# Batch 0's q and k turned by products, batch 1 scored unpaired, and the list in a new order

## The chip, the cores and the metric

The kernel runs on 1 core of one Trainium2 chip. The metric is the device time of one execution in microseconds; the runs shown are compared by their median.

## The reference

```python
def _attn_ref(q, k, v):                 # 8 batches, 8 heads, 576 tokens, 64 dims
    scores = scale * np.matmul(q, k.transpose(0, 1, 3, 2))
    mask = np.abs(pos[:, None] - pos[None, :]) <= 32
    scores = np.where(mask, scores, -1000000000.0)
...                                     # softmax over keys, times v
def _moe_ref(x, w_gate, wq, wk, wv, wo):   # x: 8 x 576 x 512, the heads side by side
    logits = x @ w_gate                    # 4 experts, the best 2 per token, softmax of these
    for e in range(4):
        q = x @ wq[e]; k = x @ wk[e]; v = x @ wv[e]     # 64 wide
        ...                                # causal attention
        ye = a @ v @ wo[e]
        ...                                # added where e is chosen, times its weight
```

So each batch has a sliding window attention of 8 heads and then a mixture of four causal attentions of one head each.

## The kernel before

The kernel is a list of some thousand steps (`ORDER`), written out by hand or by a planner, and each step is a small function that issues a few instructions. The order of the list is the order in which each engine gets its instructions; what overlaps across engines is decided by semaphores alone. A step's name holds the operation, then batch, and then what it needs: `sc210@24` is operation sc of batch 2, head group 1, half 0, with PSUM banks from 2 and from 4; a letter behind a colon names the engine of a copy (v VectorE, a ScalarE, g GpSimd) or, for products, whether the rows are split (q) or not.

The steps that matter here, for a batch b and a group g of four heads:

- `lq`, `lk`, `lv` load q, k and v. Loads go to the SP queue (f: ScalarE's queue), and `load` makes each wait for the last product ahead of it in the list. For batch 0, q and k come in two parts of 8 and 10 of the 18 tokens of a partition.
- `tq`, `tk` turn q and k with VectorE's stream transpose (line 317), in blocks of 32. Each head then has its 64 dims as two blocks of 32 rows. `mv` moves such blocks within SBUF by four DMAs (line 366), and `qc`, `kc` copy one block by an engine, so that a product can take 64 rows at once. `PAIRED` says whether that was done: a paired score block has 20 products of 64 rows, an unpaired one 40 of 32 rows.
- `hq`, `hk` turn batch 0's q and k on TensorE instead (line 193), two tokens at a time, and `iq`, `ik` copy the result from PSUM (lines 182 and 184), by 64 partitions.
- `sc` makes the scores of one half of the queries for four heads. For batches in `NBS` it adds the mask beforehand, by 8 products with the unit matrix. `ex` is the exponential (line 418). For other batches `mk` multiplies by the mask afterwards (line 422).
- `vc` copies v rows to the other 64 partitions' layout; `av` multiplies with v; `un` normalises on VectorE (lines 450 to 457); `xt` turns the result (line 193), `xf` and `xb` copy and cast it.
- `ga` to `gu` are the gate. `pp`, `pe`, `pv`, `ve` make the experts' q, k and v; `ps`, `xe`, `se` their scores, exponential and causal mask (lines 618 to 623); `po`, `oe`, `pt`, `ot` their products with v; `py`, `ye`, `st` the output.
- `wm` are dummy products, four to a step, that fill the time before data arrives (line 237).

Scores of batch b + 1 or b + 2 are interleaved by the list with the experts' work of batch b.

Of the kernel before, what the change touches and what calls it, by code (L numbers as in the profile page):

```python
# [25 lines left out]
NBS = (0, 1)  # L26
OCUT = 8

ORDER = """
    lq002:e s_mask s_ones s_fill s_ident s_warm s_pads lq001:e lk001:f lq012:e wm2@0 lk002:f lk012:f wm0@0 lq011:e  # L30
    lv02 lk011:f hq001@0 lv00 wm3@2 lv03 iq0013:v@0 lk100:e iq0012:a@0 iq0010:v@0 hq000@2 iq0003:v@2 iq0000:a@2
    iq0001:a@2 hk000@3 ik0003:a@3 iq0011:a@0 ik0002:a@3 s_nb hq011@4 iq0113:v@4 iq0110:v@4 iq0112:v@4 iq0002:v@2
    ik0001:a@3 hk001@6 wm1@0 ik0010:a@6 ik0000:v@3 hk011@0 iq0111:v@4 hq010@2 iq0100:v@2 iq0101:v@2 lv01 vc01:g
    ik0111:v@0 lq100:e ik0110:v@0 lv04 lk110:e ik0012:a@6 ik0113:v@0 lq110:e lw1 ik0013:a@6 iq0102:v@2 ik0011:a@6
    sc001@35 ex0010@3 hk010@7 ik0100:a@7 iq0103:a@2 ik0101:a@7 ik0112:v@0 ex0011@5 sc000@02 ik0103:v@7 ex0001@2
    ik0102:v@7 sc011@46 ex0110@4 sc010@24 ex0111@6 ex0101@4 lw0 av03@4 tk100:e kc10:v ex0100@2 ex0000@0 av04@0
    tq100:e un03@4 qc10:a mv10 vc00:g un04@0 lk200:e av02@2 lq200:e un02@2 lv13 xt02@4 xf02:a@4 xt01@2 av00@0
    xf01:a@2 tq110:e xb01:g xb02:g un00@0 av01@4 un01@4 xt00@4 xf00:a@4 lv10 cw0:g tk110:e sc101@02 qc11:a kc11:v
    sc100@46 mv11 tk200:e ex1010@0 ex1000@4 ex1001@6 lv11 ex1011@2 xb00:g lv12 ga0@0 gt0 gm0 ge0 cw1:g gu0@0
    pp011@4 pe011:a@4 pp010@2 lk210:e pe010:a@2 tq200:e pp000@6 ps011@2 pe000:a@6 qc20:v ps013@4 xe011@2 se011  # L40
    vc11:v pp001@0 pe001:a@0 xe013@4 kc20:g lq210:e ps010:q@6 se013 mv20 lv14 sc111@02 lq300:e xe010@6 sc110@46
    ex1111@2 tk210:e ex1110@0 ex1101@6 ps002:q@2 ps003:q@0 xe003@0 se010 ps001:q@6 ex1100@4 lw2 xe001@6 ps000:q@0
    xe000@0 vc10:g av11@4 un11@4 xe002@2 av10@6 un10@6 ps012:q@0 xe012@0 lv22 kc21:a sc201@24 se012 lk300:e
    ex2010@2 mk2010:g tq210:e cw2:g ex2011@4 qc21:a mv21 sc200@06 xt10@2 ex2001@6 xf10:a@2 tq300:e qc30:a av12@4
    av13@6 pv01@2 lv23 av14@3 xb10:g ve01:a@2 se003 ex2000@0 lq310:e un12@4 un13@6 xt11@6 xf11:a@6 xb11:a mk2011:g
    un14@3 lk310:e tk300:e kc30:g pv00@0 ve00:a@0 xt12@6 xf12:v@6 xb12:g se001 mk2001:v sc210@24 mv30 ex2100@2
    mk2000:v lv21 sc211@06 ex2111@6 lw3 lq400:e ex2110@0 mk2110:g ga1@3 ex2101@4 gt1 ge1 pv10@6 ve10:a@6 mk2101:g
    se002 gm1 gu1@3 pp100@4 tk310:e lv24 mk2111:g pe100:a@4 lv20 pp110@2 pe110:a@2 sc300@04 ex3001@4 ex3000@0 lv31
    sc301@26 tq310:e lk400:e pp101@4 ex3010@2 pe101:v@4 ex3011@6 cw3:a se000 po00@0 oe00@0 ps100@4 xe100@4 ps101@6
    xe101@6 po01@2 pt00@0 oe01@2 ot00:a@0 vc20:g qc31:g pp111@4 kc31:g mv31 pe111:a@4 lv32 lv33 ps102@6 mk2100:g  # L50
    vc21:g pt01@0 se100 ps103@1 xe103@1 xe102@6 se102 tq400:e qc40:g ps110@4 xe110@4 se110 pv11@3 ve11:a@3 av23@1
    av20@6 ot01:v@0 un23@1 mk3011:g py02@5 ye02:a@5 av24@0 lq410:e ps113@1 xe113@1 lk410:e un20@6 tk400:e ps112@4
    xe112@4 un24@0 ps111@6 xe111@6 py01:q@2 av21@4 un21@4 av22@6 un22@6 ye01:a@2 se113 sc311@02 ex3111@2 sc310@46
    tq410:e ex3110@0 kc40:g mv40 st02 mk3001:g ex3101@6 se112 ex3100@4 lk500:e mk3010:g xt20@2 xf20:a@2 xt21@0
    xf21:a@0 xt22@6 lv30 xf22:v@6 se101 se103 po10@4 oe10@4 py00@2 ye00:a@2 sc400@06 ex4000@0 st01 ex4001@6
    lq500:e mk3101:g lv42 sc401@24 xb20:g ex4011@4 se111 po11@0 lv34 lk510:e qc41:g ex4010@2 pt10@7 xb22:v xb21:g
    tk410:e pp201@5 pe201:a@5 pp200@2 kc41:a lv41 ga2@6 pe200:a@2 ps200@2 tk500:e ps203@4 st00 xe203@4 mv41 oe11@0
    ps202@0 xe202@0 xe200@2 ot10:v@7 pt11@7 ot11:a@7 gt2 pp210@4 mk3100:v mk3000:g vc31:g pe210:v@4 tq500:e
    pp211@0 mk3110:g mk3111:g av33@2 pv21@7 un33@2 vc30:g av31@4 un31@4 lq510:e mk4010:g qc50:g ve21:a@7 pe211:a@0
    ge2 lv43 av34@7 un34@7 py11:q@0 ye11:a@0 mk4001:g py10:q@2 ye10:a@2 py12@7 ye12:a@7 av30@4 gm2 gu2@6 av32@0  # L60
    xt32@6 un30@4 xf32:a@6 sc410@24 un32@0 kc50:g mv50 xb32:g lv52 mk4011:v ex4101@4 mk4101:g ex4100@2 mk4100:g
    sc411@06 ex4110@0 tq510:e qc51:g mk4110:g lk600:e lv40 xt31@4 xf31:a@4 lq600:e se200 xb31:v xt30@2 xf30:a@2
    pv20@0 ve20:v@0 ps213:q@2 ex4111@6 mk4111:g lv44 vc41:g xe213@2 se213 xb30:v tk510:e vc40:g ps212:q@4 xe212@4
    mk4000:g sc501@26 ex5010@2 ex5011@6 sc500@04 ex5000@0 lv53 mk5000:g tk600:e ex5001@4 pp300@2 pp301@0 pe300:a@2
    kc51:a se203 ps201@4 xe201@4 tq600:e pe301:a@0 ps211@2 ga3@7 xe211@2 gt3 kc60:g mv51 gm3 pp311@5 pe311:a@5
    ps210@0 xe210@0 se210 lv51 ps302@2 xe302@2 se211 pv31@4 av42@5 un42@5 ge3 ve31:a@4 vc50:g av43@0 un43@0 av40@2
    un40@2 ps301@5 xe301@5 lk610:e se301 av44@4 un44@4 qc60:a pp310@0 pe310:a@0 gu3@7 xt41@4 xf41:v@4 mk5010:g
    ps300@2 xe300@2 se202 av41@6 un41@6 ps303:q@0 sc511@24 xe303@0 mv60 se212 mk5001:v ex5110@2 ex5111@4 lq610:e
    sc510@06 lv54 lv50 mk5110:g tk610:e kc61:v lq700:e ex5101@6 ex5100@0 xt40@2 xf40:a@2 xb41:g xb40:g pv30@4
    ve30:a@4 xt42@0 xf42:v@0 sc600@26 ex6001@6 xb42:g ex6000@2 lk710:e mk5101:v sc601@04 ex6011@4 ex6010@0 lk700:e  # L70
    pp400@6 se201 po20@2 mk5011:g pe400:a@6 tq610:e qc61:g ps313@0 xe313@0 ps312@4 oe20@2 tq700:e ps311@6 xe311@6
    pp411@0 pt20@2 lq710:e xe312@4 ot20:a@2 pe411:a@0 mk5100:g po21@6 oe21@6 pp401@4 vc51:g ga4@3 mk5111:g
    pe401:a@4 ps403@6 xe403@6 ps401@4 xe401@4 ps310@0 xe310@0 tk700:e kc70:g mk6001:g pv41@2 ve41:a@2 av51@6
    un51@6 qc70:g gt4 ge4 av52@4 un52@4 av50@0 se310 pt21@2 ot21:a@2 se302 st11 un50@0 mv61 pv40@6 mv70 gm4
    ve40:a@6 xt50@4 gu4@3 mk6011:g ps402@0 av54@2 un54@2 lv60 xf50:a@4 xb50:g lv64 se401 av53@6 lv70 un53@6
    xe402@0 sc610@24 ex6100@2 lv62 ex6101@4 lv63 sc611@06 ps400:q@2 ex6111@6 xe400@2 tq710:e mk6101:g py21@4
    pp410@6 pe410:v@6 ex6110@0 ye21:a@4 lv61 st10 lv71 se402 xt51@2 xt52@0 xf52:v@0 xf51:a@2 se312 xb52:a mk6100:g
    sc701@46 ex7010@4 sc700@02 ex7001@2 xb51:v pp500@4 ex7000@0 mk6000:g tk710:e lv73 pp501@2 st12 ex7011@6 se303
    se313 se311 po31@6 oe31@6 lv72 pe501:a@2 pp511@2 pe511:v@2 st21 mk6111:g se300 po30@0 oe30@0 pe500:a@4 qc71:a
    ps503@6 ps502@4 xe503@6 mk6010:v xe502@4 ps411@2 xe411@2 vc60:g ga5@7 gt5 ps410@0 xe410@0 ps501@5 ge5 pt31@4  # L80
    ot31:v@4 pp510@2 pt30@4 pe510:v@2 mk6110:g kc71:g vc61:g py20@0 xe501@5 gm5 av61@2 av60@5 ot30:a@4 un61@2
    ye20:a@0 gu5@7 un60@5 av63@0 un63@0 av62@2 un62@2 py22@7 ye22:v@7 ps413@4 xe413@4 av64@6 mv71 sc711@04 un64@6
    ex7110@0 xt60@2 ex7111@4 se502 xt62@6 st22 lv74 xf62:v@6 xf60:a@2 xb60:v py31@0 mk7011:g sc710@46 ye31:a@0
    st31 ex7101@6 se413 mk7110:g ex7100@4 mk7100:v xt61@2 xf61:a@2 ps412@0 xe412@0 mk7111:g pv50@6 se501 st20
    se403 se400 po40@2 oe40@2 ga6@0 ve50:a@6 gt6 ps513@6 xe513@6 mk7001:g ps500@4 xb62:g ps510@2 xe500@4 pt40@1
    xb61:g xe510@2 vc71:v pp601@6 pe601:a@6 mk7000:g pp600@4 pe600:a@4 ge6 se410 ot40:v@1 se411 se412 po41@2
    pp611@4 pe611:a@4 py30@6 mk7010:g se500 ye30:a@6 pv61@1 py32@4 ye32:a@4 ve61:a@1 oe41@2 gm6 gu6@0 vc70:g
    av72@2 un72@2 ps602@6 xe602@6 ps600@4 av73@0 mk7101:g un73@0 av70@2 un70@2 xe600@4 ps603@6 ps601@4 xe603@6
    pt41@0 ot41:v@0 xe601@4 pp610@6 pe610:a@6 ps511@4 ps512@2 xe512@2 se601 se512 xe511@4 se510 st30 se503 av74@0
# [695 lines left out]
```

## Time and profile before

| | |
|---|---|
| median of 3 runs | 241.84 us (241.49 to 243.21) |
| the profiled execution: time, span | 240.19 us, 238.5 us |
| PE busy, instructions | 213.3 us (89%), 4579 |
| DVE busy | 188.1 us (79%) |
| ACT busy | 164.3 us (69%) |
| POOL busy | 144.7 us (61%) |
| DMA | 48.80 MB, mean 205 GB/s |

PE is TensorE's products, PEld its loads of weights, DVE VectorE, ACT ScalarE, POOL GpSimd. The span runs from the first to the last instruction of the profiled execution; its time has some 1.7 us more around it. The shares are means over a run whose stages differ, so a table by stretches of time says more than they do. Products are pipelined and their ends are modelled, so that a busy PE may still be issuing slowly: the count of instructions in a stretch is to be read beside the busy time.

### The profile page before, as it was taken

To read this page: it belongs to the slowest core of one execution; us is meant where nothing else is said; L and a number is where in the kernel's file an instruction comes from. 1 tells how busy PE (TensorE), PEld (TensorE's weight loads), DVE (VectorE), ACT (ScalarE), POOL (GpSimd) and SP (SyncE) were. 2 spreads that over 40 slices of the span, in tenths; PEclk is the share of its full clock that TensorE was granted. 3 is DMA by queue.
4 is the path that set the end of the run, shared out by engine and by line. 5 is a ranking of instruction groups with operands and counts; after the bars stand their busy time and mean duration, and the time that the engine had idled before them with its cause. 6 is when DMAs were issued, how large, how long until landed. Compare 5 with 4: busy or idle time off the path is not lost.

```text
span 238.5 us, 10662 instructions
## 1 busy us (share of the span) xinstructions
PE 213.3 (89%) x4579; PEld 166.9 (70%) x4588; DVE 188.1 (79%) x350; ACT 164.3 (69%) x260; POOL 144.7 (61%) x189
## 2 busy tenths in 40 slices
...
GB/s 208 289 286 304 222 279 205 280 276 252 270 240 258 236 210 324 275 233 201 287 160 185 176 322 278 166 214 197 205 16 160 55 108 4 73 133 0 201 200 198
DMA packets 57487, 48.80 MB, mean 205 GB/s; under 512 B 40544, under 2 KB 43104, under 8 KB 57440
## 3 DMA queue, kind: packets, MB, share of 16 engines
...
q10 hardware_dynamic: 576, 1.18, 1.5%
...
## 4 chain that ended last, share of the span: by engine, by line
PE 53%; DVE 14%; POOL 9%; DMA 8%; ACT 6%; issue 6%; SPq 1%; ACTq 0%; DVEq 0%; POOLq 0%
PE PS L190 49%; DMA T<-T 5%; DVE T L317 5%; PE PS L193 4%; POOL A L422 4%; DVE T L184 3%; DMA V<-in_v_dram 3%; ACT A L418 2%; ACT XTF L182 2%; POOL V L184 1%; POOL ATE L623 1%; DVE XN L451 1%; DVE OE L659 1%; SPq L196 1%; POOL XTB L184 1%
## 5 line engine op out<-in xcount | busy, mean ns | idle before, releaser
L422 POOL TENSOR_TENSOR A<-A,MASKP 128x576 f32<-128x576 f32 x40 | 57.6, 1448 | 7.7 <-ACT A L418 7.4
L623 POOL TENSOR_SCALAR_AFFINE_SELECT ATE<-ATE 128x256 bf16<-128x256 bf16 (+1 forms) x80 | 31.1, 407 | 37.2 <-ACT ATE L618 30.8
L618 ACT ACTIVATE ATE<-PS 128x1024 bf16<-128x1024 f32 x48 | 47.5, 1030 | 6.0 <-PE PS L190 6.0
L418 ACT ACTIVATE A<-PS 128x576 f32<-128x576 f32 x64 | 38.3, 653 | 16.7 <-PE PS L190 16.1
L190 PE MATMUL PS<-T 64*64 64x128 f32 (+3 forms) x1280 | 40.6, 263 | 2.7 <-DMA T<-T 1.3
L190 PE MATMUL PS<-V,A 128*64 128x65 f32 (+1 forms) x1280 | 39.5, 223 | 3.2 <-POOL V L184 1.7
L190 PEld LDWEIGHTS PS<-V,A 128*64 128x64 f32 (+1 forms) x1280 | 36.0, 132 | 7.5 <-POOL V L184 2.0
L190 PEld LDWEIGHTS PS<-T 64*64 64x64 f32 x1280 | 34.2, 133 | 6.2 <-DMA T<-T 1.4
L184 POOL COPY V<-V 64x1536 f32<-64x1536 f32 (+1 forms) x14 | 24.8, 1772 | 18.8 <-DMA kn<-in_k_dram 14.1
L317 DVE STREAM_TRANSPOSE T<-qn 128x1152 f32<-128x1152 f32 x14 | 32.6, 2329 | 4.5 <-DMA kn<-in_k_dram 1.9
L317 DVE STREAM_TRANSPOSE T<-kn 128x1152 f32<-128x1152 f32 x14 | 32.3, 2330 | 1.3 <-DMA T<-T 0.8
L451 DVE TENSOR_TENSOR XN<-PS,RC 128x512 f32<-128x512 f32 x32 | 22.1, 691 | 1.3 <-DVE RC L450 0.2
L182 ACT COPY Y<-PS 128x1024 f32<-128x1024 f32 (+1 forms) x20 | 16.7, 859 | 8.8 <-PE PS L190 5.7
L182 ACT COPY XTF<-PS 128x1024 f32<-128x1024 f32 (+1 forms) x21 | 17.2, 834 | 7.9 <-PE PS L193 6.3
L184 POOL CAST XTB<-XTF 128x128 bf16<-128x128 f32 (+1 forms) x21 | 15.5, 758 | 11.7 <-ACT XTF L182 11.3
L190 PE MATMUL PS<-WV,XTB 128*128 128x256 bf16 (+1 forms) x192 | 18.6, 256 | 2.0 <-DVE OTT L184 1.8
L190 PE MATMUL PS<-WO,OTT 128*128 128x512 bf16 (+2 forms) x99 | 18.4, 347 | 1.7 <-ACT OTT L182 1.1
L182 ACT CAST QKE<-PS 128x576 bf16<-128x576 f32 x25 | 15.9, 644 | 5.4 <-PE PS L190 5.2
L190 PE MATMUL PS<-QKE 64*128 64x64 bf16 (+9 forms) x220 | 17.9, 279 | 1.6 <-DVE OE L659 1.0
L190 PE MATMUL PS<-XTB,WK 128*128 128x288 bf16 x128 | 18.3, 286 | 0.1
L190 PE MATMUL PS<-XTB,WQ 128*128 128x288 bf16 x128 | 18.0, 286 | 0.0
L190 PEld LDWEIGHTS <-XTB 128*128 128x128 bf16 (+1 forms) x192 | 14.4, 102 | 5.1 <-issue 3.4
...
## 6 DMA issues: line engine op xcount, KB each, us to landing
...
kn<-in_k_dram SPq DMA_DIRECT2D x28, 288.0 KB, 5.4
qn<-in_q_dram SPq DMA_DIRECT2D x28, 288.0 KB, 5.1
T<-T SPq DMA_DIRECT2D x56, 144.0 KB, 4.2
...
```

Source lines behind the costliest of these rows:

```text
L182: nc.scalar.copy(o, i)
L184: eng(c).tensor_copy(o, i)
L190: last_pe[0] = nc.tensor.matmul(*a, **kw)
L193: last_pe[0] = nc.tensor.transpose(*a)
L196: r = q_.dma_start(o, i)
L317: nc.vector.transpose(T.rearrange("q h (p o) -> q h o p", o=18)[:, :, o0:o1, :], x[:, :, o0:o1, :])
L418: nc.scalar.activation(AT[(2 * b + g) % NAT_][half][p], two(b0)[:, :, 0:HS], EXP, scale=scale_att)
L422: eng(c).tensor_tensor(out=ap, in0=ap, in1=MASK[:, None, HS * half:HS * half + HS].to_broadcast([128, 2, HS]), op=MULT)
L451: nc.vector.tensor_tensor(out=XN[T // 2][:, T % 2, :].rearrange("p (t h d) -> p h t d", t=4, h=8), in0=u[:, :, 0:64].rearrange("p h (d t) ...
L618: nc.scalar.activation(chunk(A, ch), two(b0), EXP, scale=scale_moe)
L623: nc.gpsimd.affine_select(ap, ap, pattern=[[0, n], [1, w]], compare_op=IS_GE, fill=0.0, base=0, channel_multiplier=-1)
L659: nc.vector.tensor_tensor(out=O[:, :, :, :].rearrange("p t e d -> p e t d"), in0=p_[:, :, :, 0:64], in1=rg[:, :, :, None].to_broadcast([12 ...
```

## The change

The batch 0 turns become products with the unit matrix: for each token two products, of 64 columns each, put two heads into the lower and two into the upper 64 partitions of PSUM. Eight copies of 128 partitions take the place of 32 copies of 64. Batch 1 leaves `NBS`, so that its mask is applied by eight `mk` steps, and its `mv`, `qc` and `kc` steps are gone from the list, so that its scores are unpaired. The list is in another order throughout, with other engines for some copies; products without the split now carry the letter p.

```diff
-NBS = (0, 1)
+NBS = (0,)
...
     def hx(nm, b, g, ch, b0):
...
-        for n, oo in enumerate(range(4 * ch, 4 + 5 * ch)):
-            turn_pe(o[:, 128 * n:128 * n + 128], x[:, 2 * oo:2 * oo + 2, :].rearrange("p o d -> p (o d)"), ident)
+        for n, tok in enumerate(range(OCUT * ch, (OCUT, 18)[ch])):
+            for e in range(2):
+                mm(o[64 * e:64 * e + 64, 64 * n:64 * n + 64], x[:, tok, :], ident[:, 64 * e:64 * e + 64], start=True, stop=True,
+                   skip_group_check=True)
...
-    def ix(c, n, b, g, ch, k, b0):
-        e, p = k // 2, k % 2
-        m = 4 + ch
-        o = PS[64 * e:64 * e + 64, b0:b0 + 1 + ch, :].rearrange("p a x -> p (a x)")[:, 0:128 * m]
-        T = QKT[g][64 * p:64 * p + 64, 0:3:2, n, :].rearrange("q a (p oo e) -> q a p oo e", oo=9, e=2)
-        copy(c, T[:, :, :, 4 * ch:4 * ch + m, e],
-             o.rearrange("d (oo h p) -> d h p oo", oo=m, h=4)[:, 2 * p:2 * p + 2])
+    def ix(c, n, b, g, ch, b0):
+        lo, hi = ((0, OCUT), (OCUT, 18))[ch]
+        o = PS[:, b0:b0 + 1 + ch, :].rearrange("p a x -> p (a x)")[:, 0:64 * (hi - lo)]
+        T = QKT[g][:, 0:3:2, n, :].rearrange("q a (p o) -> q a p o", o=18)
+        copy(c, T[:, :, :, lo:hi], o.rearrange("d (o a p) -> d a p o", a=2, p=32))
```

The list's beginning, before and after, up to batch 0's last turn (`xt00`) and the first scores of batch 1:

```
before:
lq002:e s_mask s_ones s_fill s_ident s_warm s_pads lq001:e lk001:f lq012:e wm2@0 lk002:f lk012:f wm0@0 lq011:e
lv02 lk011:f hq001@0 lv00 wm3@2 lv03 iq0013:v@0 lk100:e iq0012:a@0 iq0010:v@0 hq000@2 iq0003:v@2 iq0000:a@2
...
sc001@35 ex0010@3 hk010@7 ik0100:a@7 iq0103:a@2 ik0101:a@7 ik0112:v@0 ex0011@5 sc000@02 ik0103:v@7 ex0001@2
ik0102:v@7 sc011@46 ex0110@4 sc010@24 ex0111@6 ex0101@4 lw0 av03@4 tk100:e kc10:v ex0100@2 ex0000@0 av04@0
tq100:e un03@4 qc10:a mv10 vc00:g un04@0 lk200:e av02@2 lq200:e un02@2 lv13 xt02@4 xf02:a@4 xt01@2 av00@0
xf01:a@2 tq110:e xb01:g xb02:g un00@0 av01@4 un01@4 xt00@4 xf00:a@4 lv10 cw0:g tk110:e sc101@02 qc11:a kc11:v
sc100@46 mv11 tk200:e ...

after:
lq001:e s_fill wm3@0 wm2@0 lq002:e s_warm s_ident lk001:f lq012:e lk002:f lk012:f lk011:f s_ones lv00 hq000@0
iq000:a@0 hq001@2 s_mask lv04 lq011:e s_nb iq001:a@2 hk000@0 ik000:a@0 lq100:e hq011@4 iq011:a@4 lv02 hk001@2
ik001:a@2 s_pads hk011@4 lv01 sc001@02 ex0010@0 ik011:v@4 lv03 ex0011@2 vc01:g sc000@46 ex0000@4 ex0001@6
tq100:e lw1 hq010@0 iq010:a@0 lk100:e tk100:e lw0 hk010@4 cw0:g ik010:a@4 sc011@02 ex0110@0 sc010@46 lk110:e
lq110:e ex0111@2 av03@2 un03@2 vc00:a av02@0 ex0100@4 un02@0 ex0101@6 av01@6 lv14 lv13 av04@5 un04@5 lq200:e
av00@2 xt02@0 xf02:a@0 un01@6 lk200:e xt01@4 xf01:a@4 xb01:g un00@2 xt00@2 xf00:a@2 xb00:g sc100@06 ex1001@6
ex1000@0 wm0@4 lv11 lv10 sc101@24 ex1011@4 ex1010@2 tk110:e lv12 xb02:g cw1:g pp010:p@0 pe010:a@0 tq110:e
...
ga0@7 mk1011:v ps013:p@0 ps010:p@5 xe013@0 mk1100:g ps011:p@3 xe011@3 wm1@2 xe010@5 pp000:p@0 mv20 pe000:a@0
...
```

More of the change, by code (lines that the diff above doesn't have):

```diff
@@ L25 @@
 NOE = 2
-NBS = (0, 1)
+NBS = (0,)
 OCUT = 8
 ORDER = """
[L30 to L89, printed above, removed]
-    un74@0 av71@6 pv51@0 un71@6 py42@1 ve51:a@0 st32 ye42:v@1 st42 xt72@2 xf72:a@2 xt71@4 xf71:a@4 xb72:g xt70@6
-    xf70:a@6 xb70:v xb71:v ps611@0 py41@2 py40@4 ye41:a@2 ye40:a@4 po50@6 xe611@0 pv60@2 ve60:a@2 pp700@0 se600
-    st41 oe50@6 ps610@6 xe610@6 pe700:v@0 se602 ps612@2 xe612@2 se513 st40 se511 po51@4 pp710@0 oe51@4 pt50@2
-    pp711@6 se611 se612 ot50:v@2 pe711:a@6 pt51@2 pe710:v@0 ot51:a@2 se603 po60@4 ps613@6 se610 xe613@6 se613
-    ps711@0 ps710@2 xe710@2 se710 xe711@0 pp701@6 pe701:a@6 oe60@4 pt60@4 po61@2 oe61@2 py50@0 ye50:a@0 st50
-    ot60:a@4 py51@6 ye51:v@6 ps702@2 py52@5 ye52:a@5 st51 pv71@0 ga7@1 ve71:v@0 gt7 xe702@2 se702 st52 ps701@6
-    ps703@2 xe703@2 ps700@4 se703 xe701@6 se701 xe700@4 pt61@0 ot61:v@0 pv70@2 gm7 py60@6 ge7 ye60:a@6 ve70:v@2
-    py61@4 st60 ye61:a@4 ps712@2 st61 xe712@2 se711 gu7@1 pw710@0 ow710@0 se700 po70@6 oe70@6 py62@4 ye62:a@4 st62
-    ps713@0 tw710@5 se712 pt70@6 ot70:v@6 pw711@7 ow711@7 uw710:a@5 py70@4 tw711@7 uw711:v@7 xe713@0 se713 pw712@6
-    ye70:a@4 st70 py71@0 ye71:a@0 st71 ow712@6 tw712@7 uw712:a@7 py72@7 ye72:v@7 st72
@@ new lines @@
+    av00@2 xt02@0 xf02:a@0 un01@6 lk200:e xt01@4 xf01:a@4 xb01:g un00@2 xt00@2 xf00:a@2 xb00:g sc100@06 ex1001@6
+    ex1000@0 wm0@4 lv11 lv10 sc101@24 ex1011@4 ex1010@2 tk110:e lv12 xb02:g cw1:g pp010:p@0 pe010:a@0 tq110:e
+    pp011:p@4 pe011:a@4 lq210:e lw2 mk1000:g tq200:e qc20:g sc110@02 ex1100@0 ex1101@2 tk200:e kc20:a mk1010:g
+    ga0@7 mk1011:v ps013:p@0 ps010:p@5 xe013@0 mk1100:g ps011:p@3 xe011@3 wm1@2 xe010@5 pp000:p@0 mv20 pe000:a@0
+    pp001:p@3 pe001:a@3 gt0 lk210:e lv24 ge0 sc111@05 ex1110@0 vc10:g vc11:g mk1001:v mk1101:v av11@3 gm0 gu0@7
@@ new lines @@
+    lv23 un11@3 lq300:e av10@0 un10@0 cw2:a ex1111@5 mk1111:g pv01@7 lk300:e ve01:a@7 sc200@24 ex2001@4 ex2000@2
+    sc201@06 ex2011@6 ex2010@0 tq210:e ps001:p@4 tk210:e xe001@4 xt10@2 lk310:e se013 mk1110:g xf10:a@2 ps000:p@6
+    xe000@6 kc21:g lv20 av12@0 un12@0 av13@4 ps012:p@2 xe012@2 se001 un13@4 av14@0 un14@0 tq300:e qc21:g mv21
+    ps002:p@6 lw3 xt11@4 xe002@6 se002 lv22 xf11:a@4 xt12@2 xf12:a@2 xb10:g xb12:g xb11:a pv00:p@0 ps003:q@4 ga1@2
+    mk2010:g tk300:e ve00:a@0 xe003@4 lv21 se003 gt1 ge1 pp100:p@6 gm1 mk2001:g pe100:a@6 gu1@2 pp101:p@4
@@ new lines @@
+    pe101:a@4 lq310:e sc210@06 sc211@24 ex2101@6 kc30:g qc30:v mv30 ex2100@0 ex2110@2 se000 se011 pp110:q@6 se010
+    ex2111@4 lq400:e tk310:e se012 po01@2 oe01@2 pe110:a@6 ps103:p@4 cw3:a xe103@4 ps102:p@6 xe102@6 lk400:e
+    po00@0 pp111:p@4 oe00@0 mk2000:g lk410:e pe111:a@4 pt01@7 mk2111:g ps101:q@2 ps100:q@0 xe101@2 tq310:e
+    ot01:v@7 pt00@6 xe100@0 pv10:p@4 ve10:v@4 ot00:a@6 lv31 mk2100:g ps113:p@0 ps110:p@2 xe113@0 mk2101:g xe110@2
+    sc300@06 ex3000@0 sc301@24 ex3001@6 ex3010@2 pv11@0 py02@1 se101 ve11:a@0 ex3011@4 lq410:e vc21:g qc31:g
@@ new lines @@
+    ps112:p@6 mk2011:v xe112@6 mk2110:g vc20:g lv33 se103 av23@2 tq400:e un23@2 py01:q@4 se102 kc31:a mv31
+    ps111:q@6 xe111@6 ye01:a@4 ye02:a@1 st02 tk400:e kc40:a se113 av24@0 se100 po10@2 oe10@2 mk3001:g av22@6 se110
+    py00:q@4 pt10@3 qc40:a un24@0 st01 un22@6 ot10:v@3 se112 se111 po11@0 oe11@0 av20@6 ye00:a@4 st00 mk3010:g
+    av21@4 un20@6 pt11@0 ot11:a@0 un21@4 mv40 sc310@26 ex3100@2 mk3011:g mk3000:v mk3100:g lk500:e sc311@04
+    tq410:e ex3101@6 ex3110@0 ex3111@4 py11:q@2 lq500:e lv30 py12@7 ye12:a@7 xt20@0 ye11:a@2 xt21@4 lv32 xf21:a@4
@@ new lines @@
+    mk3111:g qc41:g py10:q@6 xf20:v@0 xb20:g xb21:g xt22@2 xf22:v@2 lv34 ye10:a@6 lv41 xb22:a sc401@04 ex4010@0
+    mk4010:g tk410:e lv44 lk510:e sc400@26 ex4011@4 ex4000@2 pp200:q@0 pp201:q@2 ex4001@6 pp210:q@6 tk500:e
+    pe200:a@0 pp211:q@0 pe201:a@2 kc41:a pe210:a@6 ga2@2 vc31:a mk3110:g ps202:p@6 tq500:e gt2 gm2 ps200:p@3
+    pe211:a@0 mk3101:g av34@5 vc30:g av32@0 un34@5 ge2 gu2@2 un32@0 mk4011:g xe202@6 se202 mv41 xe200@3 qc50:a
+    lq510:e av31@6 av30@2 pv21@0 un31@6 kc50:g mv50 mk4001:g ve21:a@0 av33@4 xt32@6 xf32:a@6 un30@2 mk4000:g lv43
```

48 lines of the change are left out of this document (44 added, 4 removed).

## The prediction

> **What bounds the kernel now.** I read the table by stages first. Its columns are stretch and length in us, then busy us and instruction count of PE, PEld, DVE, ACT and POOL, the granted clock, the DMA share and GB/s.
>
> ```profile
> 12.00:30.00 18.00, 13.26 (x384) 11.28 (x384) 16.81 (x26) 9.57 (x18) 4.75 (x5) 1.00 0.95 272
> 30.00:60.00 30.00, 25.53 (x622) 20.94 (x622) 25.34 (x34) 23.09 (x36) 14.27 (x19) 1.00 0.99 256
> 60.00:100.00 40.00, 37.47 (x843) 29.74 (x845) 32.41 (x54) 27.41 (x44) 33.65 (x39) 1.00 0.97 257
> 100.00:180.00 80.00, 78.74 (x1864) 63.93 (x1868) 68.56 (x127) 58.27 (x95) 62.80 (x71) 1.00 0.75 204
> 180.00:200.00 20.00, 17.17 (x320) 13.47 (x314) 17.27 (x28) 14.24 (x22) 14.33 (x17) 1.00 0.27 94
> ```
>
> There are three regimes. From 12 to 30 us VectorE is busy 16.8 of 18 us (93%) while TensorE has gaps: VectorE sets the pace. From 30 to 100 us the DMA engines are full (0.97 to 0.99) and TensorE runs 622 products in 30 us and 843 in 40, or 20.7 and 21.1 per us. From 100 to 180 us it is busy 78.7 of 80 us at 23.3 per us: there TensorE is the bound and nothing is to be had from another engine. At 180 to 200 us it has gaps again (2.8 us).
>
> Then the chain that ended last (start, length, what), for which work stands in the gaps:
>
> ```profile
> 10.21 0.42 DVE T L184
> 10.64 0.50 DVE T L184
> 17.73 2.35 DVE T L317
> ...
> 30.62 0.71 PE PS L193 x16
> ...
> 42.65 6.05 DMA T<-T
> ...
> 54.42 5.57 DMA T<-T
> ...
> 178.47 2.77 POOL A L422 x2
> ...
> 191.99 2.35 POOL A L422
> ```
>
> The head is VectorE's: copies of turned q, k (L184), a stream transpose (L317), and so on until xt00, the last turn of batch 0's attention output, starts at 30.62. At 42 and 54 us the moves T<-T within SBUF stand in the chain. At 178 to 194 us it is POOL with mask products (L422). Last the waits themselves, from the timeline (start, length, engine, line, operation, and in brackets the idle time before with what ended it):
>
> ```profile
> 8.77 0.77 PE L193 MATMUL PS<-ident,qn 128*128 128x128 f32 x5 [0.72 <-DMA qn<-in_q_dram]
> 20.00 1.29 PE L190 MATMUL PS<-T 64*64 64x64 f32 x40
> 22.07 2.90 PE L190 MATMUL PS<-V,A 128*64 128x65 f32 x96 [0.78 <-ACT A L418]
> 24.21 0.21 DVE L450 RECIPROCAL RC<-PS 128x8 f32<-128x8 f32 x1
> 24.45 0.69 DVE L451 TENSOR_TENSOR XN<-PS,RC 128x512 f32<-128x512 f32 x1
> 25.27 0.42 DVE L457 TENSOR_TENSOR XN<-PS,RC 128x256 f32<-128x256 f32 x1
> 26.65 2.33 DVE L317 STREAM_TRANSPOSE T<-qn 128x1152 f32<-128x1152 f32 x1
> PE PS L190 <- DMA T<-T: 1.3, 4, 0.6
> PE PS L190 <- POOL V L184: 1.0, 1, 1.0
> ```
>
> The last two are of the table of waits of 30 to 66 us (total, times, longest).
>
> **The change part by part.** Prices first, from the groups (busy us, mean ns), the timeline, and the DMA issues:
>
> ```profile
> L184 DVE COPY T<-PS 64x320 f32<-64x320 f32 x10 | 5.0, 498 | 2.8 <-PE PS L193 2.1 <-ACT T L182 0.6
> L184 DVE COPY T<-PS 64x256 f32<-64x256 f32 x8 | 3.5, 443 | 0.7 <-ACT T L182 0.6
> L182 ACT COPY T<-PS 64x256 f32<-64x256 f32 x8 | 3.5, 439 | 1.4 <-DVE T L184 1.3
> L182 ACT COPY T<-PS 64x320 f32<-64x320 f32 x6 | 3.0, 503 | 4.4 <-DVE T L184 4.4
> L422 POOL TENSOR_TENSOR A<-A,MASKP 128x576 f32<-128x576 f32 x40 | 57.6, 1448 | 7.7 <-ACT A L418 7.4
> L422 DVE TENSOR_TENSOR A<-A,MASKP 128x576 f32<-128x576 f32 x8 | 7.7, 978 | 0.8 <-ACT A L418 0.7
> L184 DVE COPY V<-V 64x2048 f32<-64x2048 f32 x2 | 7.3, 3654 | 2.2 <-DMA V<-in_v_dram 2.2
> 12.06 0.66 PE L193 MATMUL PS<-ident,qn 128*128 128x128 f32 x4 [0.34 <-DVE T L184]
> 52.64 1.95 PEld L190 LDWEIGHTS PS<-V,A 128*64 128x64 f32 x64
> 55.03 0.50 PEld L190 LDWEIGHTS PS<-V,A 128*32 128x32 f32 x32
> 31.26 0.44 PE L190 MATMUL PS<-OTT,ident_bf 64*64 64x288 bf16 x8
> 31.41 1.04 PEld L190 LDWEIGHTS PS<-T 64*64 64x64 f32 x40
> 31.53 1.21 PE L190 MATMUL PS<-T 64*64 64x64 f32 x40
> L190 PE MATMUL PS<-T 64*64 64x160 f32 x256 | 22.8, 296 | 0.0
> 10.15 1.02 PE L237 MATMUL PS<-ATE 128*128 128x512 bf16 x4
> T<-T SPq DMA_DIRECT2D x56, 144.0 KB, 4.2
> kn<-in_k_dram SPq DMA_DIRECT2D x28, 288.0 KB, 5.4
> ```
>
> *Copies.* The 32 narrow copies go: 18 on VectorE, 8.5 us, and 14 on ScalarE, 6.5 us. Eight wide ones come, 4 of 512 and 4 of 640 elements, none in the trace. By the narrow rows an element costs (503 - 439)/64 = 1.0 ns, so 0.69 and 0.82 us. The lower bound is a narrow copy's own 0.50 us, the upper two narrow ones in sequence, 1.0. I take the middle values: 7 on ScalarE 5.2 us (-1.3) and one on VectorE 0.8 (-7.7 us, in the stage that it bounds).
>
> *Turning.* Now 36 turns; four take 0.66 us and five 0.77 (row at 8.77), so 0.11 each, 4.0 us. After it 144 f32 products of 128 rows by 64 columns, two instructions each, as the V,A products of that shape have: 1.95 us/64 = 30.5 ns each, 8.8 us. TensorE does 4.8 us more, mostly while it waited for loads or copies.
>
> *Batch 1's scores.* Its two moves go (8 of the 56 issues, 1.15 MB, 4.4 us of a full queue at 256 to 272 GB/s), with four copies T<-T; so does the mask added by products: 0.27 us ahead of each of four score blocks (31.26 to the next start, 31.53), -1.1 us. In exchange a block has 40 products of 32 rows, 80 instructions where the trace has 40 in 1.04 us, 26 ns each. Loads of 32 columns take 0.50/32 = 16 ns and of 64 columns 26 to 30, so columns count, and these have 64: 2.1 us a block, +1.04, four times +4.2 us. Bounds: 0, if four row groups run side by side as two do, and 30.5 ns, +5.6 us. I take 4.2, the row with the same operands.
> The Trainium skill, "TensorEngine Tiling (Array Packing)", section Key Properties, says that different tiles can load weights and multiply in parallel. By it the four blocks would add nothing and the sum would end 4.2 us lower; the trace's score blocks, which already alternate two row groups, load one every 26 ns and bear it out only in part.
> Eight mask products of batch 1 come instead, five on POOL (7.2 us), three on VectorE (2.9 us). On POOL the V copies of batch 1 are queued behind three of them, and av11 waits for those copies. POOL was busy 14.3 of 30 us there, so I price this at nothing; without that cover it is up to 3 x 1.45 = 4.3 us.
>
> *Fillers.* Two of the four dummy blocks (wm0, wm1) move from the loading time to behind xt00. Where TensorE sets the pace they cost 1.0 us each, +2.0; nothing, if they fall into a wait.
>
> *Elsewhere in the list.* VectorE loses two V copies (7.3 us), six of its seven XTB casts and three k copies; POOL ends about 10 us fuller over the run (six mask products, four casts, less three copies). Of batch 7's mask products POOL keeps 5 of 7, VectorE takes two more.
>
> *The head, step by step.* The third q transfer lands at 8.77. Behind it stand hq011, hk001, hk011: 60 products, 120 x 30.5 ns = 3.7 us, to 12.4. Two score blocks with masks (1.3 each): 15.0. hq010 (1.0): 16.0. Only then may batch 1's first k load (lk100) issue, for a load waits for the product ahead of it in the list; 5.4 us to landing: 21.4. Its stream transpose (2.33) holds VectorE to 23.7, and the five normalisations queue behind it: 4 x (0.21 + 0.69) + 0.6 + gaps = 4.3, so xt00 starts near 28.0 instead of 30.62: **-2.6 us**. In the kernel before, the same five were split by the stream transpose at 26.65. If lk100 lands 2.6 us later, the gain is gone.
>
> *The sum, behind xt00.* TensorE: +4.2 - 1.1 + 2.0 = **+5.1**. At 23.3 products per us the 622 and 843 of 30 to 100 us would take 26.7 and 36.2 us: 7.1 us were lost to VectorE, to moves and to V copies. VectorE is lighter there by a V copy (3.65 us) and two k copies, heavier by three mask products (2.9), and its stream transposes start earlier by the head's gain; the queue is 4.4 us lighter. I take **-4.7** back, the middle between 2.3 (the two waits of the table alone) and 7.1, since no row tells which end is nearer. POOL's stretch at 178 us is 2 x 1.45 shorter, and TensorE's gaps there are 2.8: **-1.2**, between 0 and -2.8. Together -2.6 + 5.1 - 4.7 - 1.2 = -3.4: span 238.5 to 235.1. The profiled execution has 240.19, so 1.7 around its span, and lies 1.65 under the median of the three runs, 241.84. In the median's terms: 235.1 + 3.3 = **238.4**, -1.4%.
>
> **Rivals.** *TensorE's extra instructions decide (slower).* Behind xt00 they are 5.1 to 6.5 us, in a kernel that is at 98% of TensorE for 80 us. If of the 7.1 us only the named waits (2.3) return, the stretch at 178 us returns nothing, and lk100 lands 2.6 us later so that the head gives nothing: 238.5 + 5.1 to 6.5 - 2.3 = 241.3 to 242.7, 245.3 in the median's terms. It decides once less than 5.1 us of idle TensorE disappears up to 100 us. For it: the rows of 100 to 180 us. Against it: VectorE's 93% in the head, where 7.7 us of copies go.
> *The queue is the bound and hides VectorE's relief (no change).* With a DMA share of 0.97 to 0.99 up to 100 us, batch 2's moves and V may come as late as now: only the head and the named waits return, 238.5 - 2.6 + 5.1 - 2.3 = 238.7, 242.0. For it: the chain's moves at 42 and 54 us. Against: 1.15 MB less ahead of them.
> *Four row groups run side by side (faster still).* Without the 4.2 us the sum ends at 230.9, 234.2. For it: a single instruction of 160 columns lasts 296 ns, yet the block starts one every 26 ns, so much overlaps already; against: 26 ns looks like the load of 64 columns, which would not shrink.
>
> **How the numbers follow.** A difference of 1% is about what this measurement can tell from none. Forecast 0.44, row groups 0.08: faster 0.52. No change 0.25. Slower 0.23, more than the sum gives, since the whole list is in a new order and 80 us at 98% of TensorE can only lose by that. The range, 232 to 246, runs from the row-group case with all of the 7.1 us back to the upper part of the slower one. The forecast's own is 235 to 240.
>
> **What would show it.** Right: xt00 at 27 to 29 us; VectorE busy under 14 us of 12 to 30; a score block of batch 1 at 2.0 to 2.2 us with 80 instructions; TensorE over 22 instructions per us from 30 to 100 us. Wrong: these blocks at 1.1 us (row groups) or over 2.5; VectorE idle before a transpose that waits for kn near 20 us until after 24; waits for T<-T unchanged at 45 to 60 us; av11 waiting for POOL's V copies; TensorE below 95% between 100 and 180 us, which would be the list and none of the steps priced here.

## The result: slower by 2.7%, by one copy on VectorE

The changed kernel takes 248.71 us (247.55 to 252.24, 4 runs) against 241.79 us: the ratio is 1.0267, interval 1.0209 to 1.0326. The forecast was 238.4 us and the range ended at 246. Ratios, here and below, leave out the executions that fell into a slower state. The span of the profiled execution is 245.7 us against 238.5.

The table by stages of the changed kernel, columns as before (stretch, length, busy us and count of PE, PEld, DVE, ACT, POOL, clock, DMA share, GB/s):

```profile
12.00:30.00 18.00, 14.63 (x452) 12.74 (x447) 9.11 (x13) 8.21 (x14) 3.06 (x3) 1.00 0.97 274
30.00:60.00 30.00, 28.60 (x780) 22.07 (x781) 27.84 (x37) 23.96 (x37) 21.91 (x25) 1.00 0.86 236
60.00:100.00 40.00, 34.70 (x792) 26.64 (x790) 35.52 (x46) 26.36 (x44) 28.34 (x35) 0.91 0.78 217
100.00:180.00 80.00, 76.14 (x1850) 63.85 (x1850) 66.05 (x119) 60.75 (x97) 65.17 (x72) 1.00 0.84 207
180.00:200.00 20.00, 17.38 (x342) 13.21 (x338) 17.31 (x33) 11.82 (x16) 14.93 (x20) 1.00 0.34 107
```

From 12 to 30 us VectorE fell from 16.8 to 9.1 busy us, and from 30 to 60 us TensorE ran 780 instructions instead of 622: what the change was expected to do happened. Then, from 60 to 100 us, TensorE did fewer than before (792 against 843), and the mean granted clock of TensorE is 0.91. That stretch, cut up:

```profile
65.00:70.00 5.00, 2.98 (x65) 2.26 (x61) 5.00 (x2) 3.08 (x5) 4.32 (x4) 1.00 0.24 86
70.00:75.00 5.00, 1.93 (x19) 1.11 (x20) 4.86 (x8) 0.54 (x1) 0.00 (x0) 0.59 0.77 200
75.00:80.00 5.00, 4.78 (x63) 3.56 (x65) 3.20 (x4) 3.17 (x5) 4.32 (x5) 0.72 0.81 281
```

VectorE is busy throughout 65 to 70 us with two instructions, TensorE stops, and the clock falls to 0.59 and 0.72 in the next ten microseconds. The timeline there:

```profile
61.39 0.66 POOL L184 COPY T<-T 128x576 f32<-128x576 f32 x1
61.67 7.97 DVE L184 COPY T<-T 128x576 f32<-128x576 f32 x1
62.01 1.84 POOL L623 TENSOR_SCALAR_AFFINE_SELECT ATE<-ATE 128x256 bf16<-128x256 bf16 x5
63.82 5.50 POOL L422 TENSOR_TENSOR A<-A,MASKP 128x576 f32<-128x576 f32 x4
69.56 2.32 DVE L317 STREAM_TRANSPOSE T<-kn 128x1152 f32<-128x1152 f32 x1
71.73 0.22 DVE L657 RECIPROCAL PS<-PS 128x10 f32<-128x10 f32 x1
72.19 0.82 DVE L659 TENSOR_TENSOR OE<-PS,RG 128x640 bf16<-128x640 f32 x1
73.07 0.72 PE L193 MATMUL PS<-ident_bf,OE 128*128 128x128 bf16 x5 [5.09 <-DVE OE L659]
75.34 3.09 PE L190 MATMUL PS<-WV,XTB 128*128 128x256 bf16 x16
```

The copy of 128 x 576 values is qc30, which the new list gives to VectorE (`qc30:v`). It lasts 7.97 us, where the kernel before has such copies at 0.46 to 1.77. POOL runs its own copy, five causal masks and four mask products behind one another until 69.32, and VectorE's copy ends 0.32 us later, at 69.64. Behind it wait a stream transpose and the normalisations OE, for which TensorE idles 5.09 us. The next sixteen products take 3.09 us at the low clock; 16 of the same kind took 1.92 in the kernel before.

### The profile page after: what moved, and what is told of

It is laid out like the page before. It is cut to its first block, busy times and chain, and to the rows that moved or that the text cites. A ratio compares the mean times of both kernels' runs of the same rounds, so it can differ in the third digit from the quotient of the medians.

```text
span 245.7 us, 11651 instructions
## 1 busy us (share of the span) xinstructions
PE 220.3 (90%) x5104; PEld 174.9 (71%) x5104; DVE 184.4 (75%) x326; ACT 165.6 (67%) x258; POOL 149.6 (61%) x195
## 5 line engine op out<-in xcount | busy, mean ns | idle before, releaser
L422 POOL TENSOR_TENSOR A<-A,MASKP 128x576 f32<-128x576 f32 x46 | 65.5, 1435 | 12.6 <-ACT A L418 12.1
L190 PE MATMUL PS<-V,A 128*64 128x65 f32 (+1 forms) x1280 | 41.1, 223 | 2.4 <-issue 1.6
L190 PE MATMUL PS<-T 64*64 64x128 f32 (+7 forms) x1440 | 39.5, 264 | 1.4 <-ACT XTF L182 0.6
L190 PEld LDWEIGHTS PS<-T 64*64 64x64 f32 (+1 forms) x1440 | 33.7, 132 | 4.7 <-ACT XTF L182 0.8
L184 POOL COPY V<-V 64x2048 f32<-64x2048 f32 (+1 forms) x14 | 25.0, 1788 | 15.3 <-DMA V<-in_v_dram 14.2
L184 POOL CAST XTB<-XTF 128x1024 bf16<-128x1024 f32 (+1 forms) x25 | 16.5, 682 | 13.8 <-ACT XTF L182 12.8
L190 PE MATMUL PS<-QKE 64*64 64x64 bf16 (+9 forms) x252 | 18.9, 287 | 4.9 <-DVE OE L659 2.6
L190 PE MATMUL PS<-WV,XTB 128*128 128x256 bf16 (+2 forms) x208 | 19.8, 265 | 1.1 <-DVE XN L451 1.1
L182 ACT COPY Y<-PS 128x1024 f32<-128x1024 f32 (+1 forms) x20 | 16.2, 825 | 6.2 <-PE PS L190 3.6
L190 PE MATMUL PS<-XTB,WQ 128*128 128x288 bf16 (+1 forms) x168 | 18.5, 287 | 0.1
L190 PE MATMUL PS<-XTB,WK 128*128 128x288 bf16 (+1 forms) x168 | 18.1, 287 | 0.0
```

What stands on the lines that cost most here:

```text
L182: nc.scalar.copy(o, i)
L184: eng(c).tensor_copy(o, i)
L190: last_pe[0] = nc.tensor.matmul(*a, **kw)
L422: eng(c).tensor_tensor(out=ap, in0=ap, in1=MASK[:, None, HS * half:HS * half + HS].to_broadcast([128, 2, HS]), op=MULT)
```

## The experiments

Ratios are to the kernel before, run beside each.

**e1, e2, e3: the copy on ScalarE.** The edits, e3 being both:

```diff
-... kc30:g qc30:v mv30 ...      e1
+... kc30:g qc30:a mv30 ...
-... xb60:v ...                  e2
+... xb60:a ...
```

> The changed kernel with one letter of the list changed: the copy T<-T of batch 3's q (qc30) runs on ScalarE instead of VectorE. In the changed kernel VectorE's copy lasts 7.97 us (61.67 to 69.64) while POOL runs five causal masks and four mask products back to back (62.0 to 69.3), TensorE then idles 5.1 us and its granted clock falls to 0.59 and 0.72 between 70 and 80 us. Theory A (this copy is kept out by POOL for as long as POOL's run lasts): the copy takes 0.67 us on ScalarE, the 5.1 us and the low clock go, span 245.7 down by 5 to 7, to 239 to 241, ratio to before about 1.00. Rival B (the stall belongs to the new order: TensorE would wait at the same place for something else, the moves of batch 3 or POOL): less than 2 us gained, ratio above 1.018.

> The changed kernel with the cast XTB of batch 6 (xb60) on ScalarE instead of VectorE. There it lasts 5.26 us from 185.6 beside POOL's casts and mask products, and TensorE idles 2.6 us at 192. Theory A: 2 to 3.5 us less, ratio to before about 1.015. Rival B (late waits of the list shift only): within 1 us of the changed kernel.

> Both copies on ScalarE. Theory A: the gains add, 7 to 10 us less than the changed kernel, span 236 to 239, ratio to before 0.985 to 1.00: the slowdown is these two letters of the list, and the rest of the change gains a little. Rival B: ratio still above 1.015.

Measured: e1 240.31 us, ratio 0.9944 (0.9896 to 0.9993); e2 1.0272 (1.0146 to 1.0397); e3 1.0037 (0.9982 to 1.0091). One letter is worth 3.2% of the kernel before (1.0267 - 0.9944), or some 8 us, more than the 5 to 7 us expected. In e1 the copy takes 0.66 us on ScalarE, and the stage reads:

```profile
30.00:60.00 30.00, 28.80 (x772) 21.91 (x770) 27.77 (x40) 24.01 (x38) 22.84 (x26) 1.00 0.87 244
60.00:100.00 40.00, 38.80 (x943) 30.92 (x944) 34.93 (x51) 33.32 (x53) 34.31 (x38) 1.00 0.96 256
180.00:200.00 20.00, 17.61 (x318) 13.40 (x319) 14.05 (x35) 10.17 (x16) 7.67 (x14) 0.91 0.28 93
```

```profile
61.88 0.66 ACT L182 COPY T<-T 128x576 f32<-128x576 f32 x1
```

943 instructions in 40 us instead of 792, and a full clock in that stage. The gain is more than the pause of 5.09 us, since the low clock behind it goes too: from 73.07 to 78.00 us the changed kernel has a granted clock of 0.52, which makes some 2.4 us more (an estimate: 4.93 us at 0.52). The sixteen products that end at 78.43 there end at 70.13 in e1.

The second letter gives nothing, alone or with the first; the expectation of e2 and e3 failed there. The cast xb60 is on VectorE in the kernel before too, and takes 1.29 us; in the changed kernel it takes 5.26 us, and TensorE idles 2.6 us behind it. On ScalarE the cast exchanges this pause for another. It waits for VectorE's copy of its input, the exponential behind it waits with it, and TensorE idles 2.8 us for that exponential (e2 2.81, e3 2.80, e12 2.80). The first line is from e1, the others from e12, which has the same letter:

```profile
182.39 0.64 PE L190 MATMUL PS<-QKE 64*64 64x512 bf16 x4 [2.59 <-DVE OE L659]
178.09 1.05 ACT L182 CAST XTB<-XTF 128x1024 bf16<-128x1024 f32 x1 [1.92 <-DVE XTF L184]
179.04 0.64 ACT L418 ACTIVATE A<-PS 128x576 f32<-128x576 f32 x1
179.73 1.23 PE L190 MATMUL PS<-T 64*64 64x64 f32 x40 [2.80 <-ACT A L418]
```

**e4: the same values, place and engine, another kind of instruction.**

```diff
     def qc(c, b, g):
+        if (b, g) == (3, 0):
+            nc.vector.tensor_reduce(QKT[g][:, 2, 0, :], QKT[g][:, 0, 0, :][:, :, None], axis=AXX, op=MAX)
+            return
         copy(c, QKT[g][:, 2, 0, :], QKT[g][:, 0, 0, :])
```

> The changed kernel with batch 3's q copy still on VectorE, at the same place, but issued as a maximum over an axis of length 1, which gives the same values by another kind of instruction. Theory A1 (only the f32 copy from SBUF to SBUF is kept out by POOL, other instructions of VectorE are not): 0.6 to 1 us though POOL runs beside it, time as with ScalarE, ratio about 1.00. Rival A2 (POOL keeps out any VectorE instruction that reads and writes SBUF): again 5 to 8 us, ratio about 1.027.

Measured: ratio 0.9992 (0.9932 to 1.0051). The timeline, with POOL working beside it:

```profile
62.08 0.66 POOL L184 COPY T<-T 128x576 f32<-128x576 f32 x1
62.27 0.75 DVE L356 TENSOR_REDUCE T<-T 128x576 f32<-128x576 f32 x1
62.70 1.83 POOL L626 TENSOR_SCALAR_AFFINE_SELECT ATE<-ATE 128x256 bf16<-128x256 bf16 x5
```

0.75 us instead of 7.97, and the time is that of the kernel before. It is not VectorE as such, nor any access of it to SBUF, that POOL holds up here, but the kind of instruction. The Trainium skill, "SBUF — State Buffer", section "Who interferes with whom", says so: a copy or cast of VectorE in a mode with two ports shares a port pair with GpSimd, whoever is first holds it for an instruction and the other blocks, while a reduction never contends. The trace agrees on the reduction and on the block. It goes further on its length: when the one POOL instruction that was under way at 61.67 ended at 62.05, the copy was not let in, and nine more POOL instructions passed it.

**e9: a shorter run on POOL.** The copy stays a copy on VectorE; three of POOL's four mask products move behind it.

```diff
-mk2111:g ... mk2100:g ... mk2101:g
+mk2111:v ... mk2100:v ... mk2101:v
```

> The changed kernel, qc30 still on VectorE as a copy, but POOL's run beside it shortened: three of its four mask products (mk2111, mk2100, mk2101) go to VectorE, behind the copy. Theory A (the copy waits until POOL's unbroken run ends): the run ends after five causal masks and one mask product, some 3 to 4 us after the copy's start instead of 7.7, and the copy lasts 3 to 4.5 us instead of 7.97, ending 0.3 us behind POOL's last. Rival (a fixed price of such a copy in this place, such as a slow access): 6 to 8 us again whatever POOL does.

Measured:

```profile
61.44 0.66 POOL L184 COPY T<-T 128x576 f32<-128x576 f32 x1
61.68 3.92 DVE L184 COPY T<-T 128x576 f32<-128x576 f32 x1
62.06 1.84 POOL L623 TENSOR_SCALAR_AFFINE_SELECT ATE<-ATE 128x256 bf16<-128x256 bf16 x5
63.88 1.40 POOL L422 TENSOR_TENSOR A<-A,MASKP 128x576 f32<-128x576 f32 x1
```

The copy ends at 65.60, 0.32 us behind POOL's last instruction (65.28), as it did in the changed kernel. Its length is that of POOL's run. Its one run took 242.99 us.

POOL's run is not always waited out, though. The changed kernel's other copy of this kind on VectorE (qc61) let two POOL instructions by and was then let in ahead of a third, a copy that so lasted 0.89 us, where POOL's copies of this size take 0.67:

```profile
150.10 2.37 DVE L184 COPY T<-T 128x576 f32<-128x576 f32 x1
150.76 1.40 POOL L422 TENSOR_TENSOR A<-A,MASKP 128x576 f32<-128x576 f32 x1
152.10 0.89 POOL L184 COPY T<-T 128x576 f32<-128x576 f32 x1
```

In the kernel before, four casts on VectorE (at 113.14, 115.31, 160.51 and 180.51 us, 1.11 to 1.39 us each) were let in as soon as the POOL instruction under way had ended. What decides between being let in and being passed over was not found.

**e8: the reverse, in the kernel before.**

```diff
-... lk510:e qc41:g ...
+... lk510:e qc41:v ...
```

> The reverse of the first experiment: the kernel before, with one copy T<-T (qc41) moved from POOL to VectorE, at a place where POOL runs without a gap from 83 to 93 us. Theory A (VectorE's f32 copy is kept out until POOL has a gap): the copy lasts 2 to 6 us instead of 0.6, and the time rises by 1 to 4 us, ratio 1.005 to 1.017. Rival (the changed kernel's 7.97 us had something else in it, its own order): the copy lasts under 1.8 us, ratio 1.00.

Measured: ratio 0.9955 (0.9913 to 0.9998). The time did not rise and the copy took less than the 2 to 6 us expected:

```profile
91.27 1.43 POOL L422 TENSOR_TENSOR A<-A,MASKP 128x576 f32<-128x576 f32 x1
91.56 1.45 DVE L184 COPY T<-T 128x576 f32<-128x576 f32 x1
93.62 1.89 POOL L184 COPY V<-V 64x2048 f32<-64x2048 f32 x1 [0.92 <-POOL A L422]
```

The copy began 1.1 us before the end of POOL's run, and POOL then had a gap of 0.92 us. It waited for one instruction and lasted 1.45 us, where one with POOL idle takes 0.46. Such a copy is no danger in itself; what it can cost depends on how much POOL has queued that is ready.

**e11: the same collision in the kernel before.**

```diff
-... vc71:v ...
+... vc71:a ...
```

> The kernel before with one copy of v (vc71) on ScalarE instead of VectorE. There it lasts 6.08 us from 187.0 on VectorE beside POOL's masks, and TensorE loses 2.8 us between 180 and 200 us. Theory A (the same collision costs the kernel before too): 1.5 to 3 us less, ratio 0.988 to 0.994. Rival (nothing on the path waits for it in time): ratio 0.997 to 1.003.

Measured: 239.56 us, ratio 0.9893 (0.9819 to 0.9966), as theory A had it. In the kernel before, this copy of v lets seven POOL instructions by, and is then let in ahead of a mask product of POOL, which so lasts 2.37 us (the first two lines). In e11 the copy takes 1.90 us on ScalarE and that mask product 1.39; from 180 to 200 us TensorE is busy 18.2 us instead of 17.2.

```profile
186.99 6.08 DVE L184 COPY V<-V 64x2048 f32<-64x2048 f32 x1
191.96 2.37 POOL L422 TENSOR_TENSOR A<-A,MASKP 128x576 f32<-128x576 f32 x1
186.88 1.90 ACT L182 COPY V<-V 64x2048 f32<-64x2048 f32 x1
190.45 1.39 POOL L422 TENSOR_TENSOR A<-A,MASKP 128x576 f32<-128x576 f32 x1
```

**e5, e6: each part of the change alone, in the old list.**

```diff
-hq001@0 ... iq0013:v@0 ... iq0012:a@0 iq0010:v@0 ... iq0011:a@0         e5
+hq001@0 ... iq001:a@0 ...             (hx, ix, iq, ik as after)
-NBS = (0, 1)   mv10 mv11 qc10 qc11 kc10 kc11                            e6
+NBS = (0,)     ex1011@2 mk1011:v   ex1010@0 mk1010:g   ...
```

> The kernel before, with one part of the change alone: batch 0's q and k turned by products and taken by 8 wide copies (four each on VectorE and ScalarE, at the place of the first narrow one). List, batch 1 and everything else as before. Theory: VectorE and ScalarE lose some 9 us of copies ahead of batch 1's first stream transposes, the k load of batch 1 comes as early as before, so xt00 starts 2 to 4 us earlier than 30.6 and most of that lasts to the end: ratio 0.985 to 0.993. Rival: the 4.8 us more on TensorE (or the loads) take the place of the copies: xt00 within 1 us, ratio 0.997 to 1.01.

> The kernel before, with another part alone: batch 1 unpaired, without its moves and copies T<-T and without the mask added by products; eight mask products on the engines that the changed kernel gives them (5 POOL, 3 VectorE) right behind their exponentials. Theory: a score block of 80 instructions takes 1.3 us as in the changed kernel, so TensorE pays nothing, and the waits for moves at 48 to 50 us shorten: ratio 0.99 to 0.997. Rival: the mask products on POOL hold back V copies and av11: ratio 1.00 to 1.01.

Measured: e5 1.0153 (1.0067 to 1.0239), e6 1.0474 (1.0405 to 1.0544). Both parts lose in the old list, and more than even the rivals of the two expectations allowed. In e5, as in the kernel before, seven of the eight groups of turns stand ahead of the first score block. A group of 40 instructions takes 1.16 us (9.75 to 10.91), where the old groups of 4 or 5 take 0.6 to 0.8. The score block so starts at 16.2 us instead of 12.65, and xt00 at 33.08 instead of 30.62:

```profile
9.75 1.34 PE L121 MATMUL PS<-ident,qn 128*64 128x64 f32 x40
10.91 1.34 PE L121 MATMUL PS<-ident,kn 128*64 128x64 f32 x40
16.19 0.44 PE L121 MATMUL PS<-OTT,ident_bf 64*64 64x288 bf16 x8
33.08 0.71 PE L124 MATMUL PS<-ident,XN 64*128 64x64 f32 x16 [1.10 <-DVE XN L382]
```

In e6, where each mask product was put right behind its exponential, two of them stand on POOL ahead of the cast of the weights WK. The waits of TensorE from 30 to 60 us (total, times, longest) show what that holds up; the granted clock falls there too (0.66 from 35 to 45 us):

```profile
PE PS L121 <- POOL WK L115: 2.5, 1, 2.5
PE PS L121 <- ACT A L349: 2.3, 2, 1.9
PE PS L121 <- POOL V L115: 2.3, 1, 2.3
```

**e7, e10, e12: what else the new list leaves.** All three with qc30 on ScalarE:

```diff
-... lq100:e hq011@4 ... iq010:a@0 lk100:e tk100:e ...       e7
+... lq100:e lk100:e hq011@4 ... iq010:a@0 tk100:e ...
-... ex1000@0 wm0@4 ...  ps011:p@3 xe011@3 wm1@2 ...         e10; e12 has xb60:a as well
+... ex1000@0 ...  ps011:p@3 xe011@3 ...
```

> The changed kernel with qc30 on ScalarE (as in the first experiment), and the first k load of batch 1 (lk100) moved up behind its q load, ahead of hq011. Theory: VectorE's 6.1 us wait for kn ahead of its stream transpose at 22.9 goes, un03 and its followers start at once behind av03, xt00 starts 1.5 to 3 us earlier than in the first experiment, ratio to before 0.983 to 0.99. Rival: the loads of v behind it come 1 us later, av03 waits for them instead, or TensorE's later work absorbs it: ratio as in the first experiment, 0.994.

> The changed kernel with qc30 on ScalarE and without the two dummy blocks wm0 and wm1 that the new list has behind xt00 (they compute nothing that is used). Theory: they stand where TensorE sets the pace and cost 0.6 to 1 us each; 1 to 2 us less than with them, ratio to before 0.985 to 0.992. Rival: they fall into waits for exponentials and PSUM banks, ratio 0.994 as with them.

> The changed kernel with qc30 on ScalarE, without the two late dummy blocks, and with the cast xb60 (5.25 us on VectorE beside POOL) on ScalarE too. Theory: with TensorE's other delays out of the way, the 2.6 us that TensorE idles behind xb60 near 182 us come back in part: 1 to 2.5 us less than without that letter, ratio to before 0.982 to 0.988. Rival: as in the third experiment, what is won at 182 us is lost again by 210 us, where TensorE waits for the last batch's mask products and values: ratio 0.990 to 0.994.

Measured: e7 0.9966 (0.9921 to 1.0011), e10 0.992 (0.9864 to 0.9976), e12 0.9981 (0.9943 to 1.0019). None can be told from e1's 0.9944. In e7 VectorE's wait for kn is gone, and its stream transpose starts at 18.36 us instead of 22.89 in e1. But the loads of v behind lk100 land later, POOL's copy of v starts at 21.03 instead of 18.41, and the products with v wait for it; xt00 starts at 29.08, in e1 at 29.33:

```profile
22.97 4.70 PE L190 MATMUL PS<-V,A 128*64 128x65 f32 x158 [1.42 <-POOL V L184]
```

In e12 TensorE is busy 19.68 of 20 us from 180 on, which looks like the gain hoped for from moving xb60. It is none: the pause of 2.80 us that stands in place of the old one ends at 179.73, just ahead of that stretch, and the granted clock in the stretch is 0.91. The best of all versions run is e11, the kernel before with one letter changed; its interval overlaps those of e1, e8 and e10.

## Why the prediction was wrong, point by point

**The step that failed: the list's other engines were not priced.** Under *Elsewhere in the list* the copies and casts that leave VectorE were counted, but not which ones came to it. The prediction named only that the new order could lose some of TensorE's 80 full microseconds. `qc30:v` is the one letter that decided: it stood in the sum at nothing, and the runs put it at some 8 us (e1). That such a price is possible was open to be read: of the two V copies on VectorE, whose mean of 3654 ns I quoted, one lasted 1.23 us and one 6.08, beside POOL. I took the mean for a price, and so counted the V copy that leaves VectorE ahead of 60 us at 3.65 us; it was the one of 1.23. A group of equal instructions whose mean is three times its smallest holds a wait in its busy time.

**The slower rival came true in sign, not in kind.** Two of its three conditions came: lk100 landed late and the stretch at 180 us gave nothing back. But it put the loss on TensorE's added instructions. With the letter changed, e1 has all of these and is not slower than the kernel before (0.9944), so they are paid for.

**Batch 1's scores: +4.2 us was mis-sized, near the lower bound.** The forecast was 2.1 us for the 80 loads of a block, as if their 64 columns set the pace. The trace after, the first two blocks:

```profile
30.81 1.25 PEld L190 LDWEIGHTS PS<-T 32*64 32x64 f32 x80
30.81 1.49 PE L190 MATMUL PS<-T 32*64 32x64 f32 x80
33.20 1.09 PEld L190 LDWEIGHTS PS<-T 32*64 32x64 f32 x80 [0.42 <-issue]
```

The first block takes 1.25 us, 16 ns a load, and the other three 1.09 each, 14 ns a load, against 1.04 us for 40 loads before. That is +0.4 us for the four, less than the 1.1 us that the dropped mask gives back. A single load is no shorter (131 ns on the mean, 133 for one of 64 rows), so more of them overlap: the rival of the four row groups was right on this term. The sentence of the Trainium skill's "TensorEngine Tiling (Array Packing)", Key Properties, on loads in parallel fits the measurement better than my row did.

**Turning and copies: about right.** The products cost 1.16 us for 40 (10.91 - 9.75, in e5), 29 ns each, where 30.5 was forecast. The wide copies took 0.60 and 0.70 us on ScalarE and 0.83 on VectorE, where 0.69 and 0.82 were forecast:

```profile
L182 ACT COPY T<-PS 128x512 f32<-128x512 f32 x4 | 2.4, 602 | 6.2 <-PE PS L190 6.2
L182 ACT COPY T<-PS 128x640 f32<-128x640 f32 x3 | 2.1, 702 | 1.6 <-PE PS L190 1.6
L184 DVE COPY T<-PS 128x640 f32<-128x640 f32 x1 | 0.8, 825 | 2.7 <-PE PS L190 2.7
```

**The head: -2.6 us forecast, -0.4 measured (-1.3 in e1, whose list is the same up to there).** The place was right and the landing late. lk100 was issued at 17.41, where 16.0 was forecast, and VectorE, which waited 6.6 us for it, began its stream transpose at 23.74, where 21.4 was forecast. So the normalisations and xt00 (30.17 against 30.62) came late, as the text said they would if that load landed 2.6 us later. In e7 the load comes early enough and xt00 still starts at 29.08, held up by v: the chain that was priced is not the only one that ends there.

```profile
23.74 2.34 DVE L317 STREAM_TRANSPOSE T<-kn 128x1152 f32<-128x1152 f32 x1 [6.59 <-DMA kn<-in_k_dram]
30.17 0.71 PE L193 MATMUL PS<-ident,XN 64*128 64x64 f32 x16 [0.76 <-DVE XN L451]
```

**Time taken back up to 100 us: right in direction, once the letter is changed.** In e1 TensorE runs 25.7 and 23.6 instructions per us from 30 to 60 and 60 to 100 us, over the 22 that I named. But 160 of these 1715 are the unpaired blocks' own; without them it is 22.2 per us over the 70 us, against 20.9 before. **The mask products on POOL priced at nothing** hold in the new list, where TensorE waits 0.4 us for POOL's V copies. In e6, in the old list and right behind the exponentials, the part costs some 11 us in all (4.7%), far above the 4.3 us that I gave. **The stretch at 180 us: -1.2 forecast, nothing came.** TensorE is busy 17.4 of 20 us after and 17.2 before. One pause took the place of another: 1.85 us behind the copy of v on VectorE before, 2.60 us behind the cast xb60 after. In e2 and e3 a third, of 2.8 us, stands in their place. What a shorter chain on POOL would give there was so not seen.

**Fillers: +2.0 forecast, not seen.** e10, without the two blocks, cannot be told from e1.

**What is left open.** With the terms as e1 shows them (+0.4 for +4.2, -1.3 for -2.6, nothing for -1.2) the sum would end at 237.1 in the median's terms (238.4 - 3.8 + 1.3 + 1.2). e1's ratio makes it 240.5 (0.9944 x 241.84). The 3.4 us between were not traced to a step; the time taken back is the term that no run measured by itself. That e1 comes within 1% of the forecast is so in part luck, a term too dear and others too hopeful.
